# A second level of seven products for one more unit of the output projection: small products, additions moved to GpSimd, x transposed in blocks of two tokens

## The chip, the cores and the metric

The kernel runs on one core of one Trainium2 chip. Its engines are TensorE (PE in the profile, with its weight loads as PEld), VectorE (DVE), ScalarE (ACT), GpSimd (POOL) and SyncE (SP, which only issues transfers here). The metric is the device time of one launch in microseconds (us).

## What is computed

`x` is [8, 8, 512, 64] (batch, head, token, channel) and `state` [8, 8, 32, 64]. Cut to what matters:

```python
scores = x @ state^T / 8;   a  = softmax(scores);   xread = a  @ state     # [8, 8, 512, 64]
scores2 = state @ x^T / 8;  a2 = softmax(scores2);  sread = a2 @ x         # [8, 8, 32, 64]
X = concat([xread, sread], axis=2), heads joined                          # [8 * 544, 512]
out = gelu(X @ w_in) @ w_out                                              # w_in [512, 2048], w_out [2048, 512]
```

The output is [4352, 512] in float32; the products are made in bfloat16.

## The kernel before

**The work by batches.** For each of the eight batches TensorE makes the scores (`scores`, L325; exponentials on ScalarE), the 32 state rows that read from x (`sread` L386, `reads_mm` L955), `state @ w_in` per head (`p_mm` L435), the first layer from the attention weights and that product (`mm1` L501: two matmuls of 512 columns and a Gelu on ScalarE, 16 times a batch; `M(k, k+1)` in the code is two of them), and the second layer `g @ w_out`. The state rows of all batches are carried through both layers at the end (`SR`, `R`).

**The second layer by seven products.** From batch 1 on, `g` (512 rows, 2048 inner) times `w_out` (2048, 512) is cut two by two by two and computed by seven products in place of eight, with sums of blocks of g (`g_sum`, L629, on VectorE) and of weights (`w_diff`, made once). `X(b, name)` (L672) makes one of the seven: 16 matmuls of 128x128 weights and 256 columns (L647), into the PSUM bank that `BANK` names. ScalarE copies some results out (`snap`), VectorE adds the rest into the output tiles `oh`. Product "2" of batches 2 to 7 goes down a second level: `sub_sums` (L715) forms four sums of quarter blocks on VectorE (L721), `sub_a` (L736) makes four small products (16 matmuls of 128 columns, L727) and a ScalarE copy `qa` (L741), `sub_b` (L743) makes three more on top of the same bank (12 matmuls), a ScalarE copy `qb` (L749), and three VectorE additions (L666) that form `c2`. Tiles `qa`, `qb` and `c2` exist once each.

**The order.** It is written out by hand: each engine runs its instructions in the order of the code. Batches 0 and 1 are unrolled; for b = 2 to 7 the loop has eight slots p = 0 to 7, each with `M(k, k+1)` of batch b and beside it:

- p 0: `g_sum(b-1, "56")`, `X(b-1, "1")`; GpSimd: a tiny copy `hold` that waits for a Gelu, the load of x for batch b+3, and `rearr` of batch b+2
- p 1: scores of b+1, `X(b-1, "6")`; p 2: `X(b-1, "5")`; p 3: the transposing DMA `xtr_dma` of batch b+2, `X(b-1, "7")`, `sub_sums(b)`; p 4: nothing more
- p 5: `X(b-1, "3")`, `p_all(b+1)` (`state @ w_in`, with copies on ScalarE and VectorE), `rearr_ones(b+2)` on GpSimd, `sub_a(b)`
- p 6: `sub_b(b)`; p 7: `X(b, "4")`, the closing unit, whose result ScalarE copies to `c4`

For b = 7 the slots are those of `read_out_slot` (L1027) and the tail.

**x transposed.** x of one batch lies as [token group, head, 4 tokens x 64 channels]. `rearr` (L221) copies it on GpSimd (two copies, L225) to `x4`, which pairs head c with head c+4, and `xtr_dma` (L276) transposes x4 into `xT`: a block of 128 rows is one token of two heads. Batch 1 is transposed on TensorE (`xtr`, L264). `sbd` holds state^T of a pair of heads, block by block; `state_prep` (L156) makes it by one TensorE transpose per batch and two VectorE copies (L166). `rearr_ones` (L230) makes another copy of x for the state rows.

Of the kernel before, what the change touches and what calls it, by code (L numbers as in the profile page):

```python
# [17 lines left out]
def kernel(  # L18
# [50 lines left out]
    sbd = persist.tile([128, B, HC, 2 * NS], BF16, name="sbd")  # L69
# [7 lines left out]
    sb0 = persist.tile([128, 2, 2, 2, NS], BF16, name="sb0")  # L77
    hold = persist.tile([128, 1], BF16, name="hold")
    spare = persist.tile([128, 1], FP32, name="spare")
    warm = persist.tile([128, 512], BF16, name="warm")  # L80
    xos = [persist.tile([128, SJ, HC, 132], BF16, name=f"xo_{i}") for i in range(2)]
    x4s = [persist.tile([128, SJ, HC, 128], BF16, name=f"x4_{i}") for i in range(2)]
# [12 lines left out]
    nc.gpsimd.memset(sbd, 0.0)  # L95
# [38 lines left out]
    def load_rest():  # L134
        load_w_out(4, 6)
        load_w_out(6, 8)
        load_w_in(1024, 1536)
        load_w_out(8, 12)
        load_w_in(1536, 2048)
        load_st(2, 3)  # L140
        load_x(2)
        load_w_out(12, 16)
        load_x(3)

# [11 lines left out]
    def state_prep(b0, b1, pool=ps_f, tag="f"):  # L156
        n = b1 - b0
        ps = pool.tile([128, n, HC, NS], BF16, name="st_ps", tag=tag)
        for b in range(b0, b1):
            nc.tensor.transpose(  # L160
                ps[:, b - b0, :, :].rearrange("p c n -> p (c n)"),
                st_bf[:, b, :, :].rearrange("q t d -> q (t d)"),
                ident,
            )
        for t in range(2):
            nc.vector.tensor_copy(  # L166
                out=sbd[64 * t:64 * t + 64, b0:b1, :, 32 * t:32 * t + 32].rearrange(
                    "d b c n -> d (b c) n"
                ),
                in_=ps[64 * t:64 * t + 64, :, :, :].rearrange("d b c n -> d (b c) n"),  # L170
            )
# [23 lines left out]
    def state0_p(ps):  # L195
        for t in range(2):
            h = slice(64 * t, 64 * t + 64)
            nc.scalar.copy(out=sbd[h, 0, :, 32 * t:32 * t + 32], in_=ps[h, 2, :, :])
# [7 lines left out]
    def begin(b):  # L206
        A = Att()
        atts[b] = A
        A.x4 = x4s[b % 2]
        A.xo = xos[b % 2]  # L210
        if b > 0:
            A.xT = att.tile([128, SJ, HC, 128], BF16, name="xT", tag="xT")

# [6 lines left out]

    def rearr(b, ts=(0, 1)):  # L221
        A = atts[b]
        src = xbs[b].rearrange("p (t c) (j d) -> p t c j d", t=2, d=D)
        for t in ts:
            nc.gpsimd.tensor_copy(  # L225
                out=A.x4[:, :, :, 64 * t:64 * t + 64].rearrange("p j c d -> p c j d"),
                in_=src[:, t],
            )
# [35 lines left out]
    def xtr(b, cs):  # L264
        A = atts[b]
        xv = xbs[b].rearrange("p (t c) (j d) -> p j c t d", t=2, d=D)
        ps = ps_f.tile([128, len(cs), SJ, 128], BF16, name="xT_ps", tag="f")
        for i, c in enumerate(cs):
            for j in range(SJ):
                for t in range(2):  # L270
                    nc.tensor.transpose(ps[64 * t:64 * t + 64, i, j, :], xv[:, j, c, t, :], ident)
        nc.vector.tensor_copy(
            out=A.xT[:, :, cs[0]:cs[0] + len(cs), :].rearrange("p j c n -> p c j n"), in_=ps
        )

    def xtr_dma(b):  # L276
        A = atts[b]
        nc.sync.dma_start_transpose(
            out=A.xT.rearrange("p j c n -> p (j c) n"),
            in_=A.x4.rearrange("p j c n -> p (j c n)"),  # L280
        )
# [43 lines left out]
    def scores(b, half):  # L325
        A = atts[b]
        if half == 0:
            begin_e(b)
        pt = ps_f.tile([128, SJ, 2, 2, NS], FP32, name="pt", tag="f")
        for ci in range(2):  # L330
            c = 2 * half + ci
            for j in range(SJ):
                nc.tensor.matmul(  # L333
                    pt[:, j, :, ci, :],
                    lhsT=A.xT[:, j, c, :],
                    rhs=sbd[:, b, c, :],
                    start=True,
                    stop=True,
                )
        nc.scalar.activation(  # L340
            out=A.e[:, :, 64 * half:64 * half + 64],
            in_=pt.rearrange("p j t c n -> p (j t) (c n)"),
            func=AF.Exp,
            scale=scale,
        )
# [89 lines left out]
    def p_mm(b, f, tiles):  # L435
        if b not in Ps:
            Ps[b] = att.tile([128, 2, d_ff], BF16, name="P", tag="P")
        ps = [tiles([128, 512], "p_ps") for t in range(2)]
        for c in range(HC):
            for t in range(2):  # L440
                nc.tensor.matmul(  # L441
                    ps[t][32 * c:32 * c + 32, :],
                    lhsT=sbd[64 * t:64 * t + 64, b, c, 32 * t:32 * t + 32],
                    rhs=w_in_bf[64 * t:64 * t + 64, c, f * 512:(f + 1) * 512],
                    start=True,
                    stop=True,
                )
        return ps
# [31 lines left out]
    def pmat00(h):  # L480
# [3 lines left out]
        for c in range(HC):  # L484
            for t in range(2):
                nc.tensor.matmul(
                    ps[t][32 * c:32 * c + 32, :],
                    lhsT=sbd[64 * t:64 * t + 64, 0, c, 32 * t:32 * t + 32],
# [93 lines left out]
    q_w = persist.tile([128, 4, MH // 2, QN], BF16, name="q_w", tag="mix3")  # L582

    def w_sub(k, n):
        return b21[:, MH // 2 * k:MH // 2 * k + MH // 2, QN * n:QN * n + QN]

    def w_subs(which):
        for i in which:
            x, y = (
                (w_sub(1, 1), w_sub(1, 0)),  # L590
                (w_sub(0, 1), q_w[:, 0]),
                (w_sub(0, 1), w_sub(1, 1)),
                (w_sub(0, 0), q_w[:, 1]),
            )[i]
            nc.vector.tensor_tensor(out=q_w[:, i], in0=x, in1=y, op=ALU.subtract)

    def sub_rhs(name):
        if name in "123":
            return {"1": w_sub(1, 0), "2": w_sub(0, 0), "3": w_sub(0, 1)}[name]
        return q_w[:, "5674".index(name)]  # L600
# [71 lines left out]
    def X(b, name):  # L672
# [18 lines left out]
        elif name == "5":  # L691
            snap(b, "s5", "s5", ps)
# [15 lines left out]
    def sub_q(b):  # L708
        def q(h, k):
            g = g_q(b, 0, 0)  # L710
            return g[:, MH // 2 * k:MH // 2 * k + MH // 2, 128 * h:128 * h + 128]

        return q

    def sub_sums(b):  # L715
        t = apool.tile([128, 4, MH // 2, 128], BF16, name="gsub", tag="gsum")
        got = xs[b, "sub"] = {}
        for i, name in enumerate("5673"):
            x, y, op = chain(name, sub_q(b), got)
# [3 lines left out]
    def sub_mm(b, name, at, start=False):  # L723
        lhs = chain(name, sub_q(b), {})[0] if name in "124" else xs[b, "sub"][name]
        rhs = sub_rhs(name)
        for m in range(MH // 2):
            nc.tensor.matmul(  # L727
                xs[b, 0][:, at, :],
# [7 lines left out]
    def sub_a(b):  # L736
        xs[b, 0] = otile([128, 4, QN], "xp", 0)
        for at, name in enumerate("2145"):
            sub_mm(b, name, at, at == 0)
        xs[b, "qa"] = cpool.tile([128, 4, QN], FP32, name="qa", tag="s5")  # L740
        nc.scalar.copy(out=xs[b, "qa"], in_=xs[b, 0])  # L741

    def sub_b(b):  # L743
        sub_mm(b, "6", 1)
        sub_mm(b, "3", 3)
        sub_mm(b, "7", 0, True)
        qa = xs[b, "qa"]
        qb = cpool.tile([128, 4, QN], FP32, name="qb", tag="u")
        nc.scalar.copy(out=qb, in_=xs[b, 0])  # L749
        c = xs[b, "c2"] = c_tile("c2")  # L750
        c = c.rearrange("p j (n w) -> p j n w", n=2)
        add(c[:, 0], qb[:, 1:2, :].broadcast_to([128, 2, QN]), qb[:, 0:4:3, :])
        add(c[:, 1], c[:, 0, 0:1, :].broadcast_to([128, 2, QN]), qa[:, 2:4, :])
        add(c[:, 0, 0, :], qa[:, 1, :], qa[:, 0, :])
# [28 lines left out]
    def L5():  # L783
        b = B - 1
        xs[b, "s5"] = c_tile("s5")
# [28 lines left out]
    def sr_w(name):  # L814
        if name in "52":
            homes = [opool.tile([128, 2, 512], BF16, name="srw", tag="osb") for _ in range(2)]
        elif name == "7":
            t = att.tile([128, 2, 2, 512], BF16, name="srw7", tag="xT")
            homes = [t[:, 0], t[:, 1]]
        else:  # L820
            t = x4s["16".index(name)].rearrange("p j c n -> p (j c n)")
            t = t.rearrange("p (g k f) -> p g k f", g=2, k=2)
            homes = [t[:, 0], t[:, 1]]
# [94 lines left out]
    def R(name):  # L918
        def c_new(n):
            rs[n] = cpool.tile([128, NH], FP32, name="r_" + n, tag="r_" + n)  # L920
# [106 lines left out]
    def read_out_slot(p):  # L1027
        c, b, k = B - 2, B - 1, 16 * (B - 1) + 2 * p
        if p == 0:
            sr_x("34")  # L1030
            M(k, k + 1)
            g_sum(c, "56")
# [101 lines left out]
    state_prep(1, 2)  # L1134
# [6 lines left out]
    xtr(1, (0, 1))  # L1141
    xtr(1, (2, 3))
# [19 lines left out]
    w_subs((0, 1))  # L1162
    atr(1)
    w_subs((2, 3))
# [11 lines left out]
    rearr(2)  # L1176
    xtr_dma(2)
    begin(3)
    rearr(3)
# [7 lines left out]
    state_prep(2, 3, ps_o, "o3")  # L1187
# [26 lines left out]
    M(28, 29)  # L1214
    hold_for(1, 12)
    rearr_ones(2)
    M(30, 31)
    state_prep(3, B)
# [3 lines left out]
    for b in range(2, B):  # L1222
        nb = b + 1
        for p in range(8):
# [23 lines left out]
            if b == 2 and p == 1:  # L1248
                w_diff("7")
            if p < 5 and nb < B:  # L1250
                if p == 0:
                    g_sum(b - 1, "56")
# [8 lines left out]
                if p == 3:  # L1261
                    sub_sums(b)
# [12 lines left out]
            if p == 0 and nb + 1 < B:  # L1275
                begin(nb + 1)
                rearr(nb + 1)
            if nb == B:
                if p == 5:
# [3 lines left out]
                    sub_sums(b)  # L1283
                if p == 6:
                    R("1")
                    sub_a(b)
                    R("6")
                    sub_b(b)
# [4 lines left out]
            if p == 5:  # L1293
# [11 lines left out]
                sub_a(b)  # L1305
                for _, f, ps in rest:
                    nc.scalar.copy(out=Ps[nb][:, 0, f * 512:(f + 1) * 512], in_=ps[0])
            if p == 6:
                sub_b(b)
            if p == 7:  # L1310
                if nb == B - 1:
                    srts(reads)
                X(b, "4")
# [6 lines left out]
    g_sum(b, "3", x4s[0].rearrange("p j (u c) n -> p (j u) (c n)", u=2))  # L1320
# [36 lines left out]
```

## Time and profile before

| | |
|---|---|
| median of 3 runs | 202.26 us (201.78 to 202.26) |
| the profiled execution | 202.25 us, of which the span of instructions is 200.3 us |
| granted TensorE clock | 1.000 |
| busy, share of the span | PE 97%, PEld 67%, DVE 77%, ACT 73%, POOL 24% |
| one batch in the steady part | 67.4 to 88.2, to 109.5, to 130.4, to 151.6 us: 20.8 or 21.3 us each |
| in the batch from 88.23 to 109.52 us | PE busy 21.23 us, DVE 17.12, ACT 17.32, POOL 6.50 |
| chain of work that ended last | PE 86% of the span |

A busy time is a sum over an engine's instructions; the chain is the row of steps, followed back from the last instruction, each of which released the next. Matmuls overlap one another, so the duration of one (273 ns for 256 columns) is not its price: 16 of them take 1.75 us in the chain.

### The profile page before, as it was taken

To read this page: it belongs to the slowest core of one execution; us is meant where nothing else is said; L and a number is where in the kernel's file an instruction comes from. 1 tells how busy PE (TensorE), PEld (TensorE's weight loads), DVE (VectorE), ACT (ScalarE), POOL (GpSimd) and SP (SyncE) were. 2 spreads that over 40 slices of the span, in tenths; PEclk is the share of its full clock that TensorE was granted. 3 is DMA by queue.
4 is the path that set the end of the run, shared out by engine and by line. 5 is a ranking of instruction groups with operands and counts; after the bars stand their busy time and mean duration, and the time that the engine had idled before them with its cause. 6 is when DMAs were issued, how large, how long until landed. Compare 5 with 4: busy or idle time off the path is not lost.

```text
span 200.3 us, 5055 instructions
## 1 busy us (share of the span) xinstructions
PE 193.9 (97%) x2102; PEld 134.3 (67%) x2107; DVE 155.1 (77%) x279; ACT 145.6 (73%) x264; POOL 48.1 (24%) x65
## 2 busy tenths in 40 slices
PE   7899999999999999999999999999999999999993
PEld 2533544465767777767777787677776888878893
DVE  2963796969989769975997798849966897984863
ACT  3785577699896799569966997599948778775120
POOL 8972504543403444040504300030000000000000
PEclk9999999999999999999999999999999999999999
DMA  5999999976494959680797025420024010030044
GB/s 192 197 174 202 206 199 201 183 136 142 84 149 77 241 65 164 141 214 0 77 188 209 5 67 95 138 75 27 28 107 106 0 55 0 7 153 0 18 146 157
DMA packets 40567, 23.16 MB, mean 116 GB/s; under 512 B 21856, under 2 KB 39136, under 8 KB 40544
## 3 DMA queue, kind: packets, MB, share of 16 engines
q0 software_dynamic: 13984, 8.10, 29.9%
q1 hardware_dynamic: 25728, 14.22, 27.5%
q10 hardware_dynamic: 832, 0.52, 0.8%
q8 instruction: 16, 0.26, 0.5%
q14 instruction: 7, 0.06, 0.1%
HBM read 17.30 MB, written 8.91 MB: 131 GB/s over the span
## 4 chain that ended last, share of the span: by engine, by line
PE 86%; DMA 5%; POOL 4%; ACT 2%; issue 0%; DVE 0%; POOLq 0%
PE xp L647 36%; PE hp L506 26%; DMA xb<-in_x_dram 5%; PE xp L727 5%; PE op L548 3%; PE sp L866 3%; PE rp L932 3%; POOL w_in_bf L105 2%; PE op L532 2%; PE xp L773 2%; PE pt L333 2%; ACT P L1002 1%; PE p_ps L441 1%; PE sr L962 1%; POOL sbd L95 1%; POOL w_out_bf L113 1%
## 5 line engine op out<-in xcount | busy, mean ns | idle before, releaser
L513 ACT ACTIVATE g<-hp 128x512 bf16<-128x512 f32 x124 | 67.1, 614 | 17.0 <-PE hp L506 16.8
L506 PE MATMUL hp<-AT,P 128*128 128x512 bf16 x248 | 62.2, 379 | 0.0
L647 PEld LDWEIGHTS <-gsum 128*128 128x128 bf16 x416 | 40.4, 98 | 8.9 <-issue 0.4
L647 PE MATMUL xp<-ws,gsum 128*128 128x256 bf16 x320 | 38.2, 273 | 0.0
L506 PEld LDWEIGHTS <-P 128*128 128x128 bf16 x248 | 23.0, 98 | 19.4 <-ACT P L452 0.7
L647 PEld LDWEIGHTS <-g 128*128 128x128 bf16 x240 | 23.3, 98 | 4.8
L637 DVE TENSOR_TENSOR gsum<-g 128x2048 bf16<-128x2048 bf16 x14 | 17.0, 1218 | 0.6 <-ACT g L513 0.6
L225 POOL COPY x<-xb 128x1024 bf16<-128x1024 bf16 x12 | 12.2, 1044 | 18.5 <-DMA xb<-in_x_dram 18.5
L235 POOL COPY xo<-xb 128x1024 bf16<-128x1024 bf16 x12 | 12.2, 1043 | 14.1 <-PE sr L962 13.9
L647 PE MATMUL xp<-w_out_bf,g 128*128 128x256 bf16 x128 | 15.3, 273 | 0.0
L647 PE MATMUL xp<-ws,g 128*128 128x256 bf16 x112 | 13.4, 273 | 0.0
L1016 POOL COPY hold<-g 128x1 bf16<-128x1 bf16 x7 | 2.3, 334 | 42.9 <-ACT g L513 42.9
L666 DVE TENSOR_TENSOR c<-qb 128x256 f32<-128x256 f32 x6 | 2.6, 425 | 12.7 <-ACT qb L749 12.7
L548 PE MATMUL op<-w_out_bf,g 128*128 128x512 bf16 x44 | 11.0, 380 | 0.5 <-issue 0.3
L647 PE MATMUL xp<-w_out_bf,gsum 128*128 128x256 bf16 x96 | 11.5, 273 | 0.0
L666 DVE TENSOR_TENSOR oh<-xp,c 128x512 f32<-128x512 f32 x14 | 9.6, 686 | 2.4 <-PE xp L647 2.0
L1002 DVE CAST P<-p_ps 128x512 bf16<-128x512 f32 x15 | 9.4, 683 | 2.4 <-PE p_ps L441 2.4
L356 DVE TENSOR_TENSOR a<-e,ics 128x512 bf16<-128x512 bf16 x14 | 10.5, 750 | 0.5
L353 DVE TENSOR_REDUCE cs<-e 128x16 f32<-128x512 bf16 x14 | 9.5, 678 | 0.9 <-ACT e L340 0.9
L513 ACT ACT_TABLE_LOAD x7 | 9.0, 1283 | 0.1
L441 PE MATMUL p_ps<-w_in_bf,sbd 64*32 64x512 bf16 x248 | 9.0, 380 | 0.0
L637 DVE TENSOR_TENSOR gsum<-gsum,g 128x2048 bf16<-128x2048 bf16 x7 | 8.6, 1225 | 0.2
(155 smaller groups left out, 308.9 us busy)
## 6 DMA issues: line engine op xcount, KB each, us to landing
out_dram<-oh SPq DMA_DIRECT2D x15, 256.0 KB, 3.3
xb<-in_x_dram POOLq DMA_DIRECT2D x7, 512.0 KB, 7.1
out_dram<-oh SPq DMA_DIRECT2D x6, 512.0 KB, 3.1
w_in_bf<-in_moe_w_in_dram POOLq DMA_DIRECT2D x6, 256.0 KB, 11.7
out_dram<-osb SPq DMA_DIRECT2D x5, 256.0 KB, 3.0
w_out_bf<-in_moe_w_out_dram POOLq DMA_DIRECT2D x4, 256.0 KB, 7.8
w_out_bf<-in_moe_w_out_dram POOLq DMA_DIRECT2D x2, 512.0 KB, 13.3
x0f<-in_x_dram SPq DMA_DIRECT2D x3, 256.0 KB, 3.8
```

What stands on the lines that cost most here:

```text
L225: nc.gpsimd.tensor_copy(out=A.x4[:, :, :, 64 * t:64 * t + 64].rearrange("p j c d -> p c j d"), in_=src[:, t],)
L235: eng.tensor_copy(out=A.xo[:, :, :, 2 + 64 * t:66 + 64 * t].rearrange("p j c d -> p c j d"), in_=src[:, t],)
L356: nc.vector.tensor_tensor(out=A.a[:, :, hs].rearrange("p g (c n) -> p g c n", n=NS), in0=e4, in1=ics[:, :, :].to_broadcast((128, G, 2, NS) ...
L441: nc.tensor.matmul(ps[t][32 * c:32 * c + 32, :], lhsT=sbd[64 * t:64 * t + 64, b, c, 32 * t:32 * t + 32], rhs=w_in_bf[64 * t:64 * t + 64, c ...
L506: nc.tensor.matmul(hp, lhsT=Ps[b][:, t, m * 128:(m + 1) * 128], rhs=atts[b].AT[:, :, t, :], start=(t == 0), stop=(t == 1),)
L513: nc.scalar.activation(out=gs[b][:, m, :], in_=hp, func=AF.Gelu)
L548: nc.tensor.matmul(ops[b, j], lhsT=gs[b][:, m, j * 128:(j + 1) * 128], rhs=w_out_bf[:, m, :], start=(m == 0), stop=(m == MC - 1),)
L637: nc.vector.tensor_tensor(out=got[name], in0=x, in1=y, op=op)
L647: nc.tensor.matmul(ps[:, j - js[0], :], lhsT=lhs[:, m, 128 * j:128 * j + 128], rhs=rhs[:, m, :], start=(first and j == js[0] and m == 0), ...
L666: nc.vector.tensor_tensor(out=out, in0=x, in1=y, op=ALU.add)
L727: nc.tensor.matmul(xs[b, 0][:, at, :], lhsT=lhs[:, m, :], rhs=rhs[:, m, :], start=(start and m == 0), stop=(m == MH // 2 - 1), skip_group_ ...
L1002: copy(out=Ps[b][:, t, f * 512:(f + 1) * 512], in_=ps[t])
```

## The change

Product "4" of batches 3 to 6 is made by the second level too. `sub_sums`, `sub_a` and `sub_b` take the unit as a parameter: `sub_sums(b, "4")` stands after `sub_a(b, "2")` in p 5, `sub_a(b, "4")` in p 7 where `X(b, "4")` stood, and `sub_b(b, "4")` in p 0 of the next batch, between `M(k, k+1)` and `g_sum`. Both units use the same tiles `qa` and `qb`. The additions behind `qb` are GpSimd's for both units. The weight sums of unit 4 are made once, in p 3 of batch 3.

`rearr` and `x4` are gone: `xtr_dma` transposes x as it was loaded, so a block of 128 rows is two tokens of one head. `sbd` is twice as large (a block for each head, with the same state for both tokens); each batch's state is first doubled by a copy (`state_twice`), then transposed by two transposes. For batches 4 to 7 that is done in p 4 of batch 2, with one of the two copies on ScalarE. The memory of `x4` goes to `q_w4`, `st2` and `late4`; some small tiles get other homes.

```diff
-    x4s = [persist.tile([128, SJ, HC, 128], BF16, name=f"x4_{i}") for i in range(2)]
+    late4 = persist.tile([128, 4, 512], BF16, name="late4")
...
-    nc.gpsimd.memset(sbd, 0.0)
+    nc.gpsimd.memset(sbd[:, 0:B // 2], 0.0)
...
         load_x(3)
+        nc.gpsimd.memset(sbd[:, B // 2:B], 0.0)
...
+    def state_twice(b0, b1, eng):
+        eng.tensor_copy(
+            out=st2[:, 0:b1 - b0].rearrange("q b t u d -> q (b t) u d"),
+            in_=st_bf[:, b0:b1].rearrange("q b t d -> q (b t) d")[:, :, None, :].broadcast_to(
+                [128, 2 * (b1 - b0), 2, D]
+            ),
+        )
+
+    def state_prep(b0, b1, base, pool=ps_f, tag="f"):
+        n = b1 - b0
+        ps = pool.tile([128, n, H, NS], BF16, name="st_ps", tag=tag)
+        for b in range(n):
+            for t in range(2):
+                nc.tensor.transpose(
+                    ps[:, b, HC * t:HC * t + HC, :].rearrange("p c n -> p (c n)"),
+                    st2[:, b0 - base + b, t].rearrange("q u d -> q (u d)"),
+                    ident,
+                )
+        for u in range(2):
+            copy = nc.scalar.copy if n > 1 and u else nc.vector.tensor_copy
+            copy(
+                out=sbd[64 * u:64 * u + 64, b0:b1, :, 32 * u:32 * u + 32].rearrange(
+                    "d b h n -> d (b h) n"
                 ),
+                in_=ps[64 * u:64 * u + 64, :, :, :].rearrange("d b h n -> d (b h) n"),
             )
...
+    def xtr(b, hs):
         A = atts[b]
+        ps = ps_f.tile([128, len(hs), SJ // 2, 128], BF16, name="xT_ps", tag="f")
+        for i, h in enumerate(hs):
+            for q in range(SJ // 2):
+                nc.tensor.transpose(ps[:, i, q, :], xbs[b][:, h, 128 * q:128 * q + 128], ident)
+        nc.vector.tensor_copy(out=A.xT[:, hs[0]:hs[0] + len(hs)], in_=ps)
...
-            out=A.xT.rearrange("p j c n -> p (j c) n"),
-            in_=A.x4.rearrange("p j c n -> p (j c n)"),
+            out=A.xT.rearrange("p h q n -> p (h q) n"),
+            in_=xbs[b].rearrange("p h d -> p (h d)"),
...
+    def sub_a(b, unit):
+        ps = xs[b, BANK[unit]] = otile([128, 4, QN], "xp", BANK[unit])
         for at, name in enumerate("2145"):
+            sub_mm(b, unit, name, at, at == 0)
+        xs[b, "qa"] = cpool.tile([128, 4, QN], FP32, name="qa", tag="qa")
+        nc.scalar.copy(out=xs[b, "qa"], in_=ps)
+
+    def sub_b(b, unit):
+        sub_mm(b, unit, "6", 1)
+        sub_mm(b, unit, "3", 3)
+        sub_mm(b, unit, "7", 0, True)
         qa = xs[b, "qa"]
+        qb = cpool.tile([128, 4, QN], FP32, name="qb", tag="qb")
+        nc.scalar.copy(out=qb, in_=xs[b, BANK[unit]])
+        name = "c" + unit
+        c = xs[b, name] = c_tile(name)
         c = c.rearrange("p j (n w) -> p j n w", n=2)
-        add(c[:, 0], qb[:, 1:2, :].broadcast_to([128, 2, QN]), qb[:, 0:4:3, :])
-        add(c[:, 1], c[:, 0, 0:1, :].broadcast_to([128, 2, QN]), qa[:, 2:4, :])
-        add(c[:, 0, 0, :], qa[:, 1, :], qa[:, 0, :])
+        wide = [128, 2, QN]
+        for out, x, y in (
+            (c[:, 0], qb[:, 1:2, :].broadcast_to(wide), qb[:, 0:4:3, :]),
+            (c[:, 1], c[:, 0, 0:1, :].broadcast_to(wide), qa[:, 2:4, :]),
+            (c[:, 0, 0, :], qa[:, 1, :], qa[:, 0, :]),
+        ):
+            nc.gpsimd.tensor_tensor(out=out, in0=x, in1=y, op=ALU.add)
...
-    state_prep(2, 3, ps_o, "o3")
+    state_twice(2, 3, nc.vector)
+    state_prep(2, 3, 2, ps_o, "o3")
...
+    state_twice(3, B, nc.gpsimd)
     hold_for(1, 12)
     rearr_ones(2)
     M(30, 31)
-    state_prep(3, B)
+    state_prep(3, 4, 3)
...
+            if b == 2 and p == 4:
+                state_prep(4, B, 3)
             if p < 5 and nb < B:
                 if p == 0:
+                    if b > 3:
+                        sub_b(b - 1, "4")
                     g_sum(b - 1, "56")
...
                 if p == 3:
-                    sub_sums(b)
+                    sub_sums(b, "2")
+                    if b == 3:
+                        w_subs("4", range(4))
...
-                rearr(nb + 1)
...
-                sub_a(b)
+                sub_a(b, "2")
+                if b > 2:
+                    sub_sums(b, "4")
...
             if p == 7:
                 if nb == B - 1:
                     srts(reads)
-                X(b, "4")
+                if b > 2:
+                    sub_a(b, "4")
+                else:
+                    X(b, "4")
```

## Prediction

> **What bounds the kernel now.** I read the busy times first (PE 97%), then the chain of work that ended last, then the timeline of one batch. The chain, in order of time (start, length, what), is matmuls end to end. Here are slots p 6, p 7 and p 0 around the closing unit of batch 3:
>
> ```profile
> 89.29 0.86 PE hp L506 x4
> 90.15 0.67 PE xp L727 x12
> 90.82 0.86 PE hp L506 x4
> 91.69 1.75 PE xp L647 x16
> 93.43 0.86 PE hp L506 x4
> 94.30 1.75 PE xp L647 x16
> ...
> 180.74 0.89 PE xp L727 x16
> ```
>
> No gap stands between them: TensorE waits for nobody here. So each matmul saved is saved from the end, and each new wait of TensorE is added to it. L727 x12 at 90.15 is `sub_b` of unit 2, L647 x16 at 91.69 is unit 4, the next L647 x16 is X "1"; 180.74 shows a whole `sub_a` alone. Then I asked who has no slack beside TensorE. The timeline of the same stretch (start, length, engine, line):
>
> ```profile
> 89.33 0.58 ACT L741 COPY qa<-xp 128x512 f32<-128x512 f32 x1 [0.16 <-PE xp L727]
> 89.81 1.08 ACT L1307 CAST P<-p_ps 128x512 bf16<-128x512 f32 x2
> ...
> 90.76 1.12 ACT L513 ACTIVATE g<-hp 128x512 bf16<-128x512 f32 x2
> ...
> 91.73 0.63 ACT L749 COPY qb<-xp 128x512 f32<-128x512 f32 x1
> 92.19 1.16 ACT L513 ACTIVATE g<-hp 128x512 bf16<-128x512 f32 x2
> 92.39 0.43 DVE L666 TENSOR_TENSOR c<-qb 128x256 f32<-128x256 f32 x1 [2.78 <-ACT qb L749]
> ```
>
> ScalarE runs without a gap from 89.33 to 93.35 and lies behind TensorE: `sub_b` ended at 90.82, its copy `qb` only at 92.36. Today nobody pays, since X "4" on TensorE waits for none of it.
>
> **The gain.** Unit 4 costs 1.75 us; by the second level it costs 0.89 + 0.67 = 1.56 us (rows above). Saved: 0.19 us, four times, 0.76 us. Batch 1's 32 half transposes (1.08 us in the chain, 34 ns each) become 16 whole ones at 56 ns (0.89 / 16): 0.19 us, of which I take 0.1, since the scores behind them wait for two VectorE copies of 0.69 us that stay. The scores keep 16 matmuls of 64 columns. A rule speaks against the gain: the Trainium skill, "TensorE: Matmul & The Clock Gate", section "Back-to-back issue gap", gives about 81 ns for each matmul of 128 columns in a sustained stream; 28 of them would take 2.27 us, the four units would lose 2.1 us, and the forecast would be 2.8 us higher. The row (0.89 us for 16) decides for 56 ns.
>
> **The new wait, four times.** Both units use one tile `qa`. So the ScalarE copy of `qa` for unit 4 in p 7 must wait until GpSimd's third addition of unit 2 has read the old one, and `sub_b` of unit 4 in p 0, which accumulates on the copied bank, waits for that copy. Count from T, the end of `sub_b` of unit 2 (90.82 for batch 3):
>
> - TensorE: M to T+0.86, `sub_a` of unit 4 to T+1.75, M to T+2.61. There `sub_b` of unit 4 is due.
> - ScalarE: `qb` ends at T+1.54 (the same in batches 4, 5 and 6: 113.64, 134.49, 155.72 against 112.10, 132.95, 154.19), the Gelus of p 7 at T+2.53. No earlier than that can it copy `qa` (0.58).
> - GpSimd: three additions in a row, each waiting for the one before.
>
> GpSimd's addition is in no row. Its copies are: 1024 elements in 1.044 us (L225), one element in 0.19 (L1016), so 0.83 ns an element on 0.19. With two operands read in turn, 256 elements cost 0.19 + 512 x 0.83 ns = 0.62 us and 128 cost 0.40; with one pass, 0.40 and 0.30. Below one pass I see no reason to go; nothing at all is the floor. I take two passes, an estimate nearest to that engine's rows. The skill speaks against the move too: "GPSIMD Engine Reference", section "3.1 Elementwise — side-by-side cycle accounting", measured 4497 ns for 2048 float32 elements, 2.2 ns each; with 0.19 fixed, 0.75 and 0.47 us, and by that the sum below would be 1.3 us higher.
>
> Then VectorE collides. `g_sum` "5" can start when the last Gelu has ended, T+2.57, and reads two operands from SBUF. What happens when such an instruction meets GpSimd is in this trace:
>
> ```profile
> 51.68 1.22 DVE L637 TENSOR_TENSOR gsum<-gsum,g 128x2048 bf16<-128x2048 bf16 x1
> 51.75 1.20 POOL L1016 COPY hold<-g 128x1 bf16<-128x1 bf16 x1 [1.41 <-ACT g L513]
> ```
>
> A copy of one element, 0.19 us elsewhere, takes 1.20: it ends when the VectorE sum ends. The reverse stands at 61.30, where a sum of 1.22 takes 1.83 until GpSimd's copies are through. So one holds the other off for a whole instruction. The additions: first T+1.59 to 2.21, second 2.25 to 2.86; now `g_sum` waits and takes the gap before the third, 2.86 to 4.08; third 4.08 to 4.48. `qa` 4.51 to 5.10, `sub_b` starts at 5.13: **TensorE stands 2.52 us**, four times, 10.1 us. Queued behind the waiting ScalarE copy are two Gelus and `qb`; their first users (p 1's scores and M) come 2 us later, so I charge nothing for them. `c2` itself (T+4.48) is due at X "1", T+7.5, and covered. Behind the additions on GpSimd stand `hold` and the load of x for three batches on, needed a batch later: no cost.
>
> **Stalls that come once.**
>
> - Batch 2's state: the transposes at 38.64 now wait for `state_twice` on VectorE, which stands behind the copy of U(13):
>
> ```profile
> 38.95 0.68 DVE L519 COPY osb<-op 128x512 f32<-128x512 f32 x1
> 39.55 0.45 DVE L166 COPY sbd<-st_ps 64x128 bf16<-64x128 bf16 x2
> ```
>
>  It takes the place at 39.55 and, by L235 (1024 in 0.52) and L249 (512 in 0.35), 0.26 us; TensorE goes on at 39.85 in place of 38.64: 1.2 us, and one more transpose, 0.06. In batch 1 the same wait is covered by the load of x, which ends later.
> - Batches 4 to 7, p 4 of batch 2: eight transposes, 0.44. The ScalarE half of the copy waits for the VectorE half, which stands behind `sub_sums` (ends near 65.25) and takes 0.68 (by L166: 640 in 0.48, 128 in 0.22): to 65.93. ScalarE then needs 1.0 (512 in 0.59), its two Gelus to 68.05, `sraw` 68.4, the P copy that frees bank 0 to 68.95. `sub_a` started at 67.39, now near 69.0: 1.6 us with the transposes. The first transposes (5 become 2) give back 0.17.
> - `w_subs` of unit 4 in batch 3: four sums, 0.39 apart, ahead of the addition of X "3" on VectorE. It ends near 88.7 in place of 87.37, and `p_all`'s last chunk needs its bank: `sub_a` near 89.0 in place of 88.23, 0.77 us.
>
> **At no cost:** the four sums of unit 4 on VectorE (1.6 us) fill the 2.78, 1.00 and 1.86 us of idle time ahead of today's additions, which leave; if that cover failed, `sub_a` would be late by their length. `rearr` off GpSimd and the earlier `xtr_dma` on SP: no row of TensorE waits for xT now, so nothing is won. The second half of the memset (1.8) stands where GpSimd idles 7.31 us. `state_twice` of batches 3 to 7 on GpSimd (1.3) ends near 47, a microsecond before its use at 48.47.
>
> **The sum.** -0.76 - 0.10 + 0.06 - 0.17 + 1.2 + 1.6 + 0.77 = +2.6; with 10.1, +12.7. On the profiled execution (span 200.3, 1.95 around it, 202.25; the median is 202.26): **214.9 us**.
>
> **Rivals.** *GpSimd is not interrupted* (it keeps its place while its queue is full): third addition 2.90 to 3.30, `qa` to 3.91, stall 1.33 each: 202.25 + 2.6 + 5.3 = 210.2. For it: at 96.07 two copies of GpSimd run on while a VectorE sum waits from 96.69; against it: those copies do not wait for each other, the additions do. *Additions at one pass*: they end at T+2.77, ahead of `g_sum`; `qa` to 3.38, stall 0.80: 208.1. At zero cost ScalarE alone still stalls 0.53: 207.0. *The single stalls are hidden* (3.1 us less): 211.8. *`g_sum` "6" gets in as well*, or the additions are slower still: 1.25 more each time, 219.9. *The other side*: unit 4's `qa` does not delay `sub_b`, because ScalarE is ahead rather than behind. That decides at T+2.61: if the copy has ended by then, every stall here is nil and with the single ones hidden only work counts, -0.76 - 0.10 + 0.06 - 0.17 + 0.44: 201.7, no change. It needs ScalarE 0.5 us earlier than all four batches show. That the change does not do what it says I rule out: the built program holds the 28 small matmuls at four places.
>
> **How the numbers follow.** Forecast 0.48, uninterrupted 0.20, one pass 0.12, single stalls hidden 0.07, slower still 0.08, other side 0.05. The range 207.0 to 218.5 takes in the floor of the unknown addition and a stall up to 3.4 us, and leaves out 0.13. A measurement of this kernel tells about 0.3% (0.6 us) from no change: faster 0.02, same 0.03, slower 0.95.
>
> **What would show it.** Right: before each L732 x12 in p 0 of batches 4 to 7 a gap of TensorE of about 2.5 us, released by ScalarE's `qa`, which waits for GpSimd; the third addition starting when `g_sum` ends; TensorE idle for about 1.2 us near 39. Wrong: additions of 0.4 us, `qa` beginning at T+2.5, or gaps under 1 us.

## The result and the profile after

The changed kernel takes 217.39 us (median of 4 runs, 216.95 to 218.81) against 202.06 us before: a ratio of 1.077, 95% interval 1.072 to 1.083. Forecast was 214.9 us, range 207.0 to 218.5. Medians here are over all runs of a kernel; ratios and intervals leave out two slow ones, 205.10 us of e10 and 212.25 us of e12. The profiled execution of the changed kernel took 217.81 us, its span is 216.0 us against 200.3, the granted clock 0.998.

Read its waits of TensorE first (engine, line, what it waited for: total us, times, longest us):

```profile
PE xp L732 <- ACT qa L746: 10.4, 4, 2.6
PE st_ps L171 <- DVE st L159: 1.5, 1, 1.5
PE warm_ps L152 <- DVE warm L93: 1.2, 1, 1.2
PE xT_ps L271 <- DMA xb<-in_x_dram: 0.9, 1, 0.9
PE p_ps L440 <- DVE oh L669: 0.7, 1, 0.7
```

The first row is two thirds of the 15.7 us that the span grew: four waits of 2.6 us each of `sub_b` for ScalarE's copy `qa`. The third stands in both kernels. The same view of ScalarE says why `qa` is late:

```profile
ACT qa L746 <- POOL c L764: 8.2, 4, 2.0
```

Now the chain around the closing unit of batch 3, where the chain of before was matmuls end to end (start, length, what):

```profile
94.88 0.70 PE xp L732 x12
95.58 0.45 PE hp L505 x2
96.03 0.63 ACT g L512
96.66 0.49 ACT qb L754
97.15 0.07 issue
97.23 0.73 POOL c L764
98.03 0.71 POOL c L764
98.82 1.32 POOL c L764
100.17 0.59 ACT qa L746
100.81 0.83 PE xp L732 x12
101.64 1.75 PE xp L650 x16
```

The chain leaves TensorE at 96.03 and comes back at 100.81: a Gelu, `qb`, three additions in a row on GpSimd, then `qa`. The timeline shows what those engines met:

```profile
97.23 0.72 POOL L764 TENSOR_TENSOR c<-qb 128x256 f32<-128x256 f32 x1 [2.87 <-ACT qb L754]
...
98.03 0.71 POOL L764 TENSOR_TENSOR c<-c,qa 128x256 f32<-128x256 f32 x1
98.17 1.66 DVE L640 TENSOR_TENSOR gsum<-g 128x2048 bf16<-128x2048 bf16 x1 [2.36 <-ACT g L512]
98.82 1.32 POOL L764 TENSOR_TENSOR c<-qa 128x128 f32<-128x128 f32 x1
...
100.17 0.58 ACT L746 COPY qa<-xp 128x512 f32<-128x512 f32 x1 [2.04 <-POOL c L764]
...
100.81 0.38 PE L732 MATMUL xp<-q_w,gsub 128*128 128x128 bf16 x4 [2.61 <-ACT qa L746]
```

The last row's bracket is the idle time of TensorE before it and who ended it. `g_sum` begins while the second addition runs and takes 1.66 us in place of 1.22; the third addition, the smallest, takes 1.32 and ends at 100.14, 0.31 us after `g_sum`. Without a wait the unit's `sub_b` would have begun at about 98.03, 0.86 us after the M ahead of it, as in the kernel before; so it is 2.78 us late (the bracket counts from the modelled end of the last matmul, hence 2.61).

**Where 15.7 us went**, by the starts of the same TensorE work in both chains (after minus before): the four units +10.4, net of what the smaller products save; the state of batch 2 +1.7; the eight transposes and their copies in p 4 of batch 2 +1.5; the weight sums in batch 3 +0.7; X "6" of batch 2 +0.25; the first transposes of `state_prep` -0.16. The rest belongs to transfers: the load of x for batch 1 landed 0.8 us later and the last write took 0.7 longer in this execution. The transposes behind that load start between 19.1 and 20.2 us in the thirteen traces of changed kernels, so I put this down to the execution, not to the change. Two of the other runs of the changed kernel have spans of 214.4 and 214.5 us, about that much shorter.

### The profile page after: what moved, and what is told of

Its sections match the earlier page's. It is cut to its first block, busy times and chain, and to the rows that moved or that the text cites. A ratio compares the mean times of both kernels' runs of the same rounds, so it can differ in the third digit from the quotient of the medians.

```text
span 216.0 us, 5198 instructions
## 1 busy us (share of the span) xinstructions
PE 195.7 (91%) x2141; PEld 134.8 (62%) x2146; DVE 157.6 (73%) x284; ACT 148.9 (69%) x269; POOL 63.6 (29%) x85
## 4 chain that ended last, share of the span: by engine, by line
PE 59%; DMA 12%; POOL 11%; DVE 7%; ACT 7%; issue 2%; POOLq 0%
PE xp L650 26%; PE hp L505 16%; DMA w_out_bf<-in_moe_w_out_dram 12%; POOL c L764 7%; PE xp L732 6%; PE sp L879 3%; PE rp L951 3%; ACT g L512 3%; POOL w_in_bf L106 2%; DVE oh L669 2%; PE xp L783 2%; ACT qa L746 1%; DVE gsub L725 1%; DVE P L452 1%; DVE ws L575 1%
## 5 line engine op out<-in xcount | busy, mean ns | idle before, releaser
L512 ACT ACTIVATE g<-hp 128x512 bf16<-128x512 f32 x124 | 67.2, 614 | 19.3 <-PE hp L505 19.1
L505 PE MATMUL hp<-AT,P 128*128 128x512 bf16 x248 | 62.3, 379 | 0.0
L650 PEld LDWEIGHTS <-gsum 128*128 128x128 bf16 x416 | 40.4, 98 | 9.2 <-issue 0.8
L650 PE MATMUL xp<-ws,gsum 128*128 128x256 bf16 x320 | 38.2, 273 | 0.1
L505 PEld LDWEIGHTS <-P 128*128 128x128 bf16 x248 | 22.7, 98 | 18.9 <-issue 0.6
L640 DVE TENSOR_TENSOR gsum<-g 128x2048 bf16<-128x2048 bf16 x14 | 19.2, 1369 | 13.0 <-ACT g L512 12.9
L764 POOL TENSOR_TENSOR c<-qb 128x256 f32<-128x256 f32 x10 | 7.2, 725 | 57.9 <-ACT qb L754 57.9
L669 DVE TENSOR_TENSOR oh<-xp,c 128x512 f32<-128x512 f32 (+1 forms) x22 | 14.2, 664 | 12.5 <-PE xp L650 9.7
L732 PE MATMUL xp<-q_w,gsub 128*128 128x128 bf16 x120 | 11.6, 219 | 10.4 <-ACT qa L746 10.4
L650 PEld LDWEIGHTS <-g 128*128 128x128 bf16 x176 | 17.0, 98 | 2.7
L732 PEld LDWEIGHTS <-gsub 128*128 128x128 bf16 x160 | 10.2, 98 | 13.3 <-issue 12.0
L650 PE MATMUL xp<-w_out_bf,g 128*128 128x256 bf16 x128 | 15.3, 273 | 0.0
L746 ACT COPY qa<-xp 128x512 f32<-128x512 f32 x10 | 5.9, 585 | 11.1 <-POOL c L764 8.2
L650 PE MATMUL xp<-w_out_bf,gsum 128*128 128x256 bf16 x96 | 11.5, 273 | 0.0
L440 PE MATMUL p_ps<-w_in_bf,sbd 64*32 64x512 bf16 x248 | 10.1, 381 | 1.1 <-DVE oh L669 0.7
L355 DVE TENSOR_TENSOR a<-e,ics 128x512 bf16<-128x512 bf16 x14 | 9.8, 698 | 0.5
L640 DVE TENSOR_TENSOR gsum<-gsum,g 128x2048 bf16<-128x2048 bf16 x7 | 9.3, 1331 | 0.5
```

Of the source, the lines that this page charges most:

```text
L355: nc.vector.tensor_tensor(out=A.a[:, :, hs].rearrange("p g (c n) -> p g c n", n=NS), in0=e4, in1=ics[:, :, :].to_broadcast((128, G, 2, NS) ...
L440: nc.tensor.matmul(ps[t][32 * c:32 * c + 32, :], lhsT=sbd[64 * t:64 * t + 64, b, HC * t + c, 32 * t:32 * t + 32], rhs=w_in_bf[64 * t:64 * ...
L505: nc.tensor.matmul(hp, lhsT=Ps[b][:, t, m * 128:(m + 1) * 128], rhs=atts[b].AT[:, :, t, :], start=(t == 0), stop=(t == 1),)
L512: nc.scalar.activation(out=gs[b][:, m, :], in_=hp, func=AF.Gelu)
L640: nc.vector.tensor_tensor(out=got[name], in0=x, in1=y, op=op)
L650: nc.tensor.matmul(ps[:, j - js[0], :], lhsT=lhs[:, m, 128 * j:128 * j + 128], rhs=rhs[:, m, :], start=(first and j == js[0] and m == 0), ...
```

## The experiments

The kernel before ran beside every set, with a median of 201.9 to 202.1 us; ratios are to it. Each is the changed kernel with the edit shown.

**e1: a `qa` tile for each unit.**

```diff
-    st2 = persist.tile([128, B - 3, 2, 2, D], BF16, name="st2")
+    st2 = persist.tile([128, B - 3, 2, 2, D], BF16, name="st2", tag="mix4")
...
-        xs[b, "qa"] = cpool.tile([128, 4, QN], FP32, name="qa", tag="qa")
+        xs[b, "qa"] = (
+            cpool.tile([128, 4, QN], FP32, name="qa", tag="qa")
+            if unit == "2"
+            else persist.tile([128, 4, QN], FP32, name="qa4", tag="mix4")
+        )
```

(The new tile takes the memory of `st2`, the doubled state, which is read for the last time in batch 2.)

> Only the tile: unit 4's ScalarE copy qa gets memory of its own (where the doubled state lay, which is read for the last time in batch 2). Theory of the wait (TensorE stands before sub_b of unit 4 because qa of unit 4 waits for GpSimd's third addition of unit 2): the copy then waits for ScalarE alone, sub_b starts near T+3.1 in place of T+5.2, about 2.1 us less in each of four batches: about 209 us. Rival, GpSimd's additions and their clashes with VectorE cost the time wherever they stand: within 2 us of 217.4. Rival, the transposed blocks and the doubled state cost the time: within 1 us of 217.4.

Measured 208.01 us (ratio 1.028, 1.024 to 1.033): 9.4 us of the loss were the shared tile. The timeline of e1 has the third addition as slow as before, and `qa` no longer behind it:

```profile
96.98 0.67 ACT L750 COPY qa<-xp 128x512 f32<-128x512 f32 x1
...
97.70 0.38 PE L732 MATMUL xp<-q_w,gsub 128*128 128x128 bf16 x4 [0.47 <-ACT qa L750]
...
97.86 1.32 POOL L768 TENSOR_TENSOR c<-qa 128x128 f32<-128x128 f32 x1
```

So the 1.32 us alone cost TensorE nothing here; it was the path through the tile that made them count. What is left is ScalarE's own lateness, 0.47 us.

**e2: `g_sum` held back until the third addition is done** (a VectorE copy of one element of `c2` ahead of it, at both places).

```diff
+                    if b > 3:
+                        nc.vector.tensor_copy(out=spare, in_=xs[b - 1, "c2"][:, 0, 0:1])
                     g_sum(b - 1, "56")
```

> One more instruction on VectorE: a copy of one element of c2 ahead of g_sum 5 in slot 0 of batches 4 to 7, so that g_sum starts only when GpSimd's third addition has ended. Theory that g_sum's two SBUF inputs hold the third addition off for a whole instruction: the additions take 0.72, 0.72 and 0.46 us in a row, qa ends near T+4.3 in place of T+5.2, about 0.9 us less in each of four batches: 213.5 to 214.5 us, although VectorE does more and starts later. Rival, the third addition is slow by itself or GpSimd does not mind VectorE: 217.4 or more, since g_sum comes a microsecond later.

Measured 213.83 us (1.059, 1.054 to 1.063). Its timeline:

```profile
98.26 0.45 POOL L764 TENSOR_TENSOR c<-qa 128x128 f32<-128x128 f32 x1
98.75 0.59 ACT L746 COPY qa<-xp 128x512 f32<-128x512 f32 x1 [1.17 <-POOL c L764]
98.75 0.15 DVE L1279 COPY spare<-c 128x1 f32<-128x1 f32 x1 [3.50 <-POOL c L764]
98.82 1.21 DVE L640 TENSOR_TENSOR gsum<-g 128x2048 bf16<-128x2048 bf16 x1
...
99.39 0.38 PE L732 MATMUL xp<-q_w,gsub 128*128 128x128 bf16 x4 [1.75 <-ACT qa L746]
```

Apart from each other, the addition takes 0.45 and `g_sum` 1.21 us; together they took 1.32 and 1.66. That the two hold each other off is shown, and it is 0.9 us of each stall.

**e3: all additions back on VectorE.**

```diff
-            nc.gpsimd.tensor_tensor(out=out, in0=x, in1=y, op=ALU.add)
+            nc.vector.tensor_tensor(out=out, in0=x, in1=y, op=ALU.add)
```

> The three additions behind qb go back to VectorE for both units; all else as in the changed kernel, the shared qa too. Theory of the wait: they end near T+2.8 (0.46, 0.46 and 0.29 us), qa near T+3.4, the stall of TensorE falls from 2.75 to about 0.8 us in four batches: about 209.5 us. Rival, VectorE has no room for them and g_sum comes late for X 6: 214 or more.

Measured 218.28 us (1.082, 1.076 to 1.087): my expectation failed and the rival held. The waits for `qa` did fall to 0.9 us each, but the time came back in other places, at X "6" (L650) and in the read-out slot (L879):

```profile
PE xp L650 <- DVE oh L669: 5.9, 3, 2.0
PE xp L732 <- ACT qa L746: 3.6, 4, 0.9
PE sp L879 <- DVE srt L900: 1.9, 1, 1.9
```

On VectorE unit 4's additions stand ahead of `g_sum` and wait for `qb` of p 0; its timeline shows that wait at the head of the queue, and `g_sum` could start only at 100.30:

```profile
99.17 0.42 DVE L764 TENSOR_TENSOR c<-qb 128x256 f32<-128x256 f32 x1 [2.29 <-ACT qb L754]
```

**e12: only unit 2's additions on VectorE**, to see whether it was that queue place.

```diff
-            nc.gpsimd.tensor_tensor(out=out, in0=x, in1=y, op=ALU.add)
+            eng = nc.vector if unit == "2" else nc.gpsimd
+            eng.tensor_tensor(out=out, in0=x, in1=y, op=ALU.add)
```

> The changed kernel with the three additions of unit 2 on VectorE (as before the change) and those of unit 4 on GpSimd; everything else, the shared qa tile too, as changed. Theory: e3 lost only because it put unit 4's additions ahead of g_sum in VectorE's queue; unit 2's alone stand where VectorE idles. So qa is free near T+2.8, TensorE waits 0.94 us before each sub_b (as e3 showed) in place of 2.6 to 2.8, X 6 waits for nothing, and the addition in X 6 of batch 3 no longer stands behind the load of x: 217.4 - 4 x 1.8 - 0.25 = 209.9. Rival: the additions on VectorE push g_sum back in any case, X 6 waits 1 us or more for it, and the time stays above 213.

Measured 209.97 us (1.040, 1.035 to 1.044), waits for `qa` 3.6 us in four, none of X "6". (The X "6" meant is batch 2's, made during batch 3.) The three additions end at 97.11 on VectorE, where it idled, and `g_sum` follows directly. So unit 2's additions cost 7.4 us on GpSimd (8.4 by the spans of the two profiles, 216.0 and 207.6), through the shared tile. In this order of the code, moving unit 4's additions off VectorE was right, moving unit 2's was not; unit 4's on VectorE but behind `g_sum` was not tried.

**e4: unit 4 as one product again**, its sums and weight sums gone, the rest of the change kept.

```diff
-                    if b > 3:
-                        sub_b(b - 1, "4")
...
-                    if b == 3:
-                        w_subs("4", range(4))
...
-                if b > 2:
-                    sub_sums(b, "4")
...
-                if b > 2:
-                    sub_a(b, "4")
-                else:
-                    X(b, "4")
+                X(b, "4")
```

(and `sub_b` out of `read_out_slot`.)

> Unit 4 of batches 3 to 6 as one product X again, without its sums and its weight sums; the transposed blocks, the doubled state and unit 2's additions on GpSimd stay. Theory that the four waits before sub_b are two thirds of the loss: 10.4 us and the 0.7 us of the weight sums go: about 206.3 us, 4 above the kernel before, which is the price of the single stalls. Rival, the blocks and the state cost most: 211 or more.

Measured 205.58 us (1.018, 1.013 to 1.024): what e4 keeps of the change (the layout of x^T, the way its state blocks are made, unit 2's additions on GpSimd) costs 3.5 us without unit 4. In the profiled execution the wait for `state_twice` was 2.3 us long, and the VectorE sums ahead of it had waited 1.17 us for the transfer of `w_out` (0.61 in the changed kernel).

**e5: e1, and `sub_b` of unit 4 behind X "1".**

```diff
                 if p == 0:
-                    if b > 3:
-                        sub_b(b - 1, "4")
                     g_sum(b - 1, "56")
...
                     X(b - 1, "1657"[p])
+                if p == 0 and b > 3:
+                    sub_b(b - 1, "4")
```

(and the same in `read_out_slot`.)

> Unit 4 keeps its own qa tile (as in e1) and, in p 0 of batches 4 to 7, its sub_b stands behind X 1 instead of ahead of it. Theory: what e1 left is ScalarE's own lateness, 0.47 us before each sub_b (its qa copy ends behind two Gelus); with 1.75 us of matmuls between, it is hidden four times: 208.0 - 1.9 = 206.1. Rival: the additions of unit 4 move back by some 1.8 us as well and meet the second g_sum and X 1's addition on VectorE; X 6 then waits for g_sum 6, by 0.3 to 0.5 us each time, and the time stays at 207.5 to 208. The wait before L732 and before L650 of X 6 tells them apart.

Measured 207.62 us (1.028, 1.025 to 1.030), where 206.1 was expected. The waits for `qa` are gone, as the theory had it, but their time did not come back, and not for the rival's reason either. The late `sub_b` delays `qb` on ScalarE, and behind `qb` stand the table load and the exponentials of the next batch's scores (batch 5 of e5, ScalarE):

```profile
121.17 0.58 ACT L758 COPY qb<-xp 128x512 f32<-128x512 f32 x1 [1.13 <-PE xp L732]
121.78 1.28 ACT L339 ACT_TABLE_LOAD   x1
123.07 1.08 ACT L339 ACTIVATE e<-pt 128x512 bf16<-128x512 f32 x2
124.17 1.28 ACT L512 ACT_TABLE_LOAD   x1
125.47 1.09 ACT L512 ACTIVATE g<-hp 128x512 bf16<-128x512 f32 x2
```

ScalarE stands 1.13 us for the late `sub_b`, the Gelu begins at 125.47, 0.84 us later than in e1, and TensorE waits 1.0 us for it at L423. In the read-out slot it waits 0.6 us at L883 for VectorE's `srt`, a wait that e1 doesn't have; what made it is not shown.

**e9: e1, and `sub_a` of unit 4 ahead of M in p 7** instead.

```diff
+            if p == 7 and 2 < b < B - 1:
+                sub_a(b, "4")
             if late:
                 M(k)
...
-                if b > 2:
-                    sub_a(b, "4")
-                else:
+                if b == 2:
                     X(b, "4")
```

> e1 (own qa tile), and in p 7 of batches 3 to 6 sub_a of unit 4 stands ahead of M instead of behind it; sub_b stays ahead of X 1. Theory: ScalarE then copies qa ahead of the two Gelus of p 7, near T+2.1, and is done before sub_b is due at T+2.6; the four waits of 0.47 us that e1 left go, and unlike in e5 no copy of qb stands in front of the exponential's table load: 208.0 - 1.9 = 206.1. Rival: the Gelus of p 7 end 0.6 us later, g_sum 5 and 6 with them, and X 6 waits for g_sum 6: 206.1 + 4 x 0.3 = 207.3 or more.

Measured 206.35 us (1.020, 1.016 to 1.023), as expected: no wait for `qa` is left. The rival shows too, but smaller: X "6" of batches 3 to 5 takes 1.90, 1.86 and 1.87 us in the chain in place of 1.75, and in batch 6 TensorE waits 0.3 us for a Gelu.

**e6, e7, e8: the stalls that come once**, each taken away on top of e5.

```diff
e6:
+    state_twice(2, 3, nc.vector)
     w_diff("5")
...
-    state_twice(2, 3, nc.vector)
     state_prep(2, 3, 2, ps_o, "o3")
e7:
-        for u in range(2):
+        for u in (1, 0) if n > 1 else (0, 1):
             copy = nc.scalar.copy if n > 1 and u else nc.vector.tensor_copy
e8:
-                    if b == 3:
-                        w_subs("4", range(4))
...
-            if p == 6 and b == 2:
+            if p == 7 and b == 2:
                 hold_for(b, 12)
                 load_x(5)
...
+                    w_subs("4", range(4))
                     X(b, "4")
```

> e5, and state_twice of batch 2 on VectorE ahead of w_diff instead of behind the copy of U(13). Theory: the transposes near 39 wait for that copy alone, 1.4 to 1.5 us in the changed kernel; the copy now runs in VectorE's 0.6 us of idle time ahead of w_diff, and the wait goes: e5 less 1.4, near 204.7. Rival: the two sbd copies behind the transposes or the load of x for batch 2 were nearly as late, and scores(2) takes the wait over: e5 less 0.3.

> e5, and of the two copies of state_prep(4, 8) ScalarE's comes first, VectorE's second. Theory: ScalarE idles 2.2 us there only because its half waits for VectorE's, which stands behind sub_sums; with the order turned, ScalarE copies at once, its Gelus keep their places, and p_all waits no more: e5 less 1.1, near 205.0 (of the 1.5 us that this stage lost, 0.44 are the eight transposes, which stay). Rival: p_all then waits for X 3's addition on VectorE, 0.7 us further back behind its half: e5 less 0.5.

> e5, and the four weight sums of unit 4 in p 7 of batch 2, where VectorE idles 2.7 us, instead of p 3 of batch 3; and the load of x for batch 5 with its hold behind the additions of batch 2 on GpSimd instead of ahead of them. Theory: the 0.7 us that TensorE stands before the last chunk of p_all in batch 3 go, and 0.25 us before X 6 in batch 3: e5 less 0.95, near 205.1. Rival: the sums then push g_sum 5 of batch 2 back, X 6 waits for it, and half of it comes back: e5 less 0.4.

Measured 206.92 (205.63 to 207.39), 206.93 (206.46 to 207.35) and 207.44 us (206.01 to 207.66) against 207.62 (207.41 to 208.25) for e5. The medians move less than expected, and runs of one kernel are up to 1.8 us apart, so one by one they settle little. The traces settle the stages. In e6 the wait for `state_twice` (1.4 us in e5) is no longer listed. In e7 ScalarE copies its half at 65.19 without a wait, and the stretch from X "5" of batch 1 to X "6" of batch 2 takes 19.00 us against 20.06. In e8 the wait for `oh` (0.7) is gone, and the stretch from X "6" of batch 2 to X "1" of batch 3 takes 16.95 us against 17.79. The profile of e8 has a wait that e5 lacks, 0.5 us of X "4" of batch 1 for VectorE (see e11 below). Together they were expected to bring 3.45 us, and e10 shows them together.

**e10: e9 with the edits of e6, e7 and e8. e11: e4 with those of e6, e7 and of the load of x.**

> e9 and the edits of e6, e7 and e8 together: every wait that the change brought and that the traces name is taken away. Theory: 206.1 - 1.4 - 1.1 - 0.95 = 202.6; what the change saves (0.76 us of matmuls) and what it adds in work (eight transposes, 0.44) nearly cancel, and the time is that of before within 0.5%. Rival, that the layout and the small products save more than the trace of before shows: 201.4 or less, under the kernel before.

> e4 (unit 4 one product again, no sums for it) with the edits of e6, e7 and e8: what the change to the layout of x^T costs and brings by itself. Theory: 205.6 - 1.4 - 1.1 - 0.25 = 202.8; e10 stands 0.2 to 0.8 under it, which is all that the second level of unit 4 is worth (four times 0.19 us). Rival: the second level still costs something in hidden places (VectorE and ScalarE fuller), and this run is not slower than e10.

Measured: e10 202.95 us (1.0028, 1.0003 to 1.0053), within the 0.5% that was expected, e11 203.26 us (1.0041, 1.0020 to 1.0062). From e9 to e10 3.40 us went. With the named waits gone, all of the loss is accounted for but the last 0.8 us, and what should have been gained is still not there. The chain of e10 around the closing unit of batch 4 says why:

```profile
111.51 1.56 PE xp L732 x28
113.08 1.73 PE hp L505 x8
114.80 0.67 PE xp L732 x12
115.47 1.75 PE xp L650 x16
117.22 0.47 PE pt L332 x16
117.69 0.86 PE hp L505 x4
118.55 1.86 PE xp L650 x16
```

The 28 matmuls at 111.51 are `sub_b` of unit 2 and `sub_a` of unit 4: 56 ns each, as forecast, and unit 4 costs 1.56 us in place of 1.75. But X "6" at 118.55 takes 1.86 in place of 1.75: it adds to the bank of X "1", whose VectorE addition, behind a later `g_sum`, ends at 118.45. (`g_sum` begins 0.24 us ahead of X "1" here, 0.78 in the kernel before: it waits for the last Gelu, which comes later with e9's order.) From X "1" of one batch to the next e10 needs 21.24 and 20.78 us, the kernel before 21.28 and 20.85: 0.04 and 0.07 us of the 0.19 arrive. In batch 6 TensorE also waits 0.28 us for a Gelu at L505. Over all four batches nothing is left of the gain. From `sub_a` of unit 2 in batch 3 to the last product it is 105.50 us in e10, 105.48 in e11, which has unit 4 whole, and 105.52 in the kernel before; here are the ends of that stretch in the chains of e10 (first two lines) and e11:

```profile
88.33 1.05 PE xp L732 x16
193.83 3.55 PE xp L787 x48
88.89 1.05 PE xp L732 x16
194.37 3.55 PE xp L783 x48
```

e10 and e11 are not told apart by their intervals. The 0.56 us by which e11's profile is behind at batch 3 come for the most part from a wait of 0.47 us, of X "4" of batch 1 for VectorE's copy `P`. Ahead of that copy a VectorE product (L355) took 1.39 us in place of 0.69 while GpSimd ran `state_twice` for batches 3 to 7, which waits for the state's transfer to land; e8 has the same (1.44), in e10 the two hardly met (0.74). What the last 0.8 us in the median of e10 are is open (that collision may be part of them in other runs, which no trace shows): the spans of the two profiled executions, 200.4 and 200.3 us, do not show them.

## Why the prediction was right, step by step

The forecast was 2.5 us short of the median: 1.0 lies in the four waits and some 0.6 in the single terms below. The rest lies in no term of the sum; in the profiled execution the two transfers alone moved 1.5 us.

- **The new wait, four times 2.52 us: right in mechanism, 0.26 too small.** `sub_b` was 2.78 us late (98.03 to 100.81). e1 shows the tile, e2 the collision with `g_sum`, e12 GpSimd's part. Two sizes were wrong and cancelled, which is luck. An addition takes 0.72, 0.71 and 0.45 us where nothing disturbs it, against my 0.62, 0.62 and 0.40; the estimate took a copy's slope twice. But from the end of the second to the end of the third, with `g_sum` between, it is 1.40 us against my 1.62. So the three take 2.91 us from first start to last end, against 2.89. The 0.26 are about 0.10 at the handovers between engines and 0.16 that I had left out: behind a wait `sub_b`'s 12 matmuls take 0.83 us in the chain, not 0.67. For the addition alone, what I worked out from the price in the Trainium skill ("GPSIMD Engine Reference", section "3.1 Elementwise — side-by-side cycle accounting"), 0.75 and 0.47 us, was the nearer estimate.
- **The interruption: right.** It was the likeliest case against "not interrupted" (210.2) and "one pass" (208.1); 1.32 us in the trace, 0.45 in e2. `g_sum` took the place ahead of the third addition, as forecast.
- **The gain, 0.76 us: right for the matmuls** (28 in 1.56 us), and hidden in the changed kernel behind the stalls. With the stalls gone, e10 shows that it is lost again, at X "6" and at a Gelu in batch 6; that I had not seen.
- **Batch 1's transposes, 0.1 us: wrong, nil.** 16 whole ones take 1.07 us in the profile, 32 half ones took 1.08, both behind a wait. I had set the 1.08, measured behind a wait, against 0.89, measured without one; in e11, where no wait stands ahead of them, the 16 take 0.89.
- **State of batch 2, 1.26 us with its transpose: right place, 0.4 too small** (1.7). VectorE's sums ahead of the copy waited 0.61 us for the transfer of `w_out`, 0.24 in the kernel before; I had kept the 0.24.
- **p 4 of batch 2, 1.6 us: right** (1.5); e7 shows the order of the two copies as the cause of all but the transposes' 0.45.
- **`w_subs`, 0.77 us: right** (0.7, and gone in e8).
- **Missed: X "6" of batch 2, 0.25 us.** I had looked at the additions of unit 2 only where the next unit waits for them. In batch 2 they stand behind the load of x for batch 5 on GpSimd, collide with both `g_sum`, and VectorE's addition for X "1" waits for them; e12 has them on VectorE and shows no such wait.
- **Missed in part: `state_twice` of batches 3 to 7 on GpSimd.** It ends near 47 as forecast (46.98), but at no cost only where it does not meet VectorE: 0.5 us of TensorE in the profiles of e8 and e11.
- **The other side (ScalarE ahead, 201.7): wrong as a picture of this change.** The kernel that it comes nearest to is e10 (202.95), where that wait and the single ones are taken away: nothing is won then.

## What to carry to other kernels

- When one tile serves two units, count the wait from its last reader on the slowest engine, and price that reader in the company it will have: 0.45 us alone became 1.32 beside a large VectorE sum.
- On an engine that runs in order, an instruction that waits at the head of the queue costs whoever stands behind it (e3's additions ahead of `g_sum`, e5's `qb` ahead of the table load); asking where an operation stands was worth 8 us between e3 and e12.
- A saving of 0.19 us in a unit that is one link of a chain is worth its measured share only when the next waiters are looked at too: with the named stalls removed, 0.04 and 0.07 of it arrived in two batches, and over all four nothing.

## What the runs showed of the hardware

- A GpSimd addition of two float32 operands takes 0.72 us for 256 elements and 0.45 for 128 in these traces: 2.1 ns an element on some 0.18, against 0.83 ns for a bfloat16 copy in the trace of before.
- Between two GpSimd additions of which one waits for the other, a VectorE sum of two operands got in, and the next addition ended 0.3 us after that sum: 0.45 us became 1.32 (after, e1), 1.31 (e5), 1.36 (e9). One of 256 elements that met the second `g_sum` took 1.71 us and ended 0.59 after it (e9).
- 16 whole transposes on TensorE take as long as 32 half ones: 1.07 and 1.08 us, both behind a wait.
